# A fused attention, mixer and two-layer feed-forward kernel: where the norm's small steps keep the variance, and which engine rounds the streamed weights

## The chip, the cores and the metric

One core of one Trainium2 chip runs the whole program in one launch. The metric is the device time in microseconds. Before the change three runs took 1761.98, 1762.68 and 1764.5 us, a median of 1762.68 us.

## What is computed

The inputs are `q`, `k`, `v` of shape 8 x 8 x 576 x 64 and two sets of feed-forward weights (512 to 2048 to 512). Cut to what matters here:

```python
x  = attention(q, mean8(k), mean8(v))           # per head; to 8 x 576 x 512
u  = x + token_mixer(x, U, V)
x1 = u + relu(u @ w1a) @ w2a                    # first layer
mu, var = mean(x1), mean((x1 - mu) ** 2)        # over the 512 features of a token
xn = (x1 - mu) / sqrt(var + 1e-6) * g
return x1 + relu(xn @ w1b) @ w2b                # second layer
```

The result has to match in float32. Matrix products run on operands that are split into a rounded part (type `fp32r`, the "hi" part) and the rest ("lo"): hi x hi, hi x lo and lo x hi are summed, so every operand costs a rounding copy (hi) and a subtraction (lo).

## The kernel before, in words

The 4608 tokens are 9 groups of 512. After the attention and the first half of the first layer (the trace's first 605 us or so), three passes run: pass 0 is the second half of the first layer, passes 1 and 2 are the two halves of the second layer. A pass goes over the 9 groups, and a group over 4 pairs of weight blocks; one (pass, group, pair) is a unit (`unit`, lines 1504 to 1590). A unit forms its 512 x 512 product by Strassen-like sums of seven 256-column products, called p1, p5, p6, p2, p3, p7, p4 in the order in which they run; all matmuls of these stand at L1519. Products p1, p6, p7 and p4 go to a PSUM bank `pa`, and p5, p2 and p3 to a bank `pbc`. Between them copies `s` are taken out of the banks (`snap`, L404 on ScalarE or L406 on VectorE), VectorE adds `s` back (L1577 into `pbc`, L1583 into `pa`), and `hidden` writes the relu to `hid` (ScalarE L1541, VectorE L1547). p2 can't write `pbc` before the copy `s` of p5 has been read from it, and p4 can't write `pa` before L1583 has read p7 from it. The second product of the previous unit (`second`, L1607, banks `py`) is put between these seven as filler. There are two `pa` banks, two `pbc` banks and four `py` banks.

While pass 0 runs over group g, the norm of group g-1 is computed in steps n0 to n3 (`norm`, lines 1694 to 1775); the last group's norm falls into the first group of pass 1. n1 subtracts the mean (L1742) and stores the tokens in HBM (`n_d`). n2 squares. n3 sums the squares over the features with four 2-column matmuls into a `pbc` bank (L1731), and then has small steps on 128 x 4 values: the square root (ScalarE, L1759, tile `lnd`), variance plus 1e-6 (VectorE, L1760, tile `lnv`), a reciprocal (L1761), and one correction of 1/sqrt, `r*(1.5 - 0.5*v*r*r)`: two products (L1763), a scale-and-add (L1764) and a product (L1765). The 512 factors are then stored token by token in HBM (L1769, `r_d`, 4 bytes each). Pass 2 needs them.

The weights of a pass are 4 pairs. They are fetched in `load_pair` (lines 1401 to 1459): two DMAs (L1417) bring the first matrices of a pair into the one buffer `wraw`, four sums and differences are formed (L1435, GpSimd or VectorE), and `split` (lines 546 to 558) makes the hi parts `w1h` (a copy: L404 on ScalarE, L406 on VectorE) and the lo parts `w1l` (L555, VectorE or GpSimd); the same follows for the second matrices (`w2h`, `w2l`) through the same buffer. Pairs of the next pass are fetched while the last group of this pass and the first of the next one run. In the first groups of pass 1, raw 8-byte weights of later blocks are also fetched (L737, `wraw<-wC`), decoded (L593 to L620), scaled and stored (L766), as background.

The order of all instructions on all engines is written out ahead by a list scheduler in the program (`Order.schedule`, lines 151 to 320): it simulates the five engines with a cost for each operation, gives an operation to one of the engines that it names (`engs`), and takes the oldest ready one first. Where VectorE and GpSimd both work on SBUF alone, it lets them exclude each other (`o.port`: an operation that touches no PSUM buffer). SyncE issues all of these DMAs, in that order too. Each engine works through its list in order, and waits at the head of it on semaphores.

Of the kernel before, what the change touches and what calls it, by code (L numbers as in the profile page):

```python
# [13 lines left out]
AF = mybir.ActivationFunctionType  # L14
ALU = mybir.AluOpType
# [15 lines left out]
TG = 512  # L31
# [19 lines left out]
class Ring:  # L51


    def __init__(self, pool, shape, dtype, n, name, fifo=True):
        self.pool, self.shape, self.dtype, self.n, self.name, self.fifo = pool, shape, dtype, n, name, fifo
        self.tiles, self.free, self.made, self.turn = None, [(0.0, i) for i in range(n)], 0, 0
        pool.rings.append(self)
# [34 lines left out]
PE, ACT, DVE, GP, SY = "pe", "act", "dve", "pool", "sync"  # L92
# [262 lines left out]
CW = 2  # L355
# [23 lines left out]
def c_pool(n):  # L379
    return 147 + 2.11 * n  # L380
# [42 lines left out]
class Kern:  # L423
    def __init__(self, nc, tc, aps):
        self.nc, self.tc = nc, tc
        (self.qT, self.kT, self.v, self.U, self.V, self.wA, self.g, self.wC, self.out) = aps
        self.w_raw = [self.wA, self.wC]
        self.o = Order(nc, tc)
        att = Pool("att")
        stg = Pool("stg")  # L430
        slots = Pool("slots", side="right")
        w = Pool("wres", side="right")
        b1 = Pool("b1", after=[att])
        b2 = Pool("b2", side="right", after=[w])
        ps = Pool("ps", space=PSUM)
        self.pools = [stg, att, slots, w, ps, b1, b2]
        R = self.R = {}

        def ring(pool, name, shape, dt=F32, n=1, fifo=True):
            R[name] = Ring(pool, shape, dt, n, name, fifo)  # L440

        ring(stg, "wraw", [128, 512], I64)
        ring(stg, "wx", [128, 512])
        ring(stg, "wt", [128, 512])
        ring(att, "araw", [128, 512], I64)
        ring(att, "ax", [128, 512])
        ring(att, "at", [128, 512])
        ring(att, "kbd", [128, 2, SP], n=2)
        ring(att, "q", [128, S], n=2)
        ring(att, "k", [128, S])  # L450
        ring(att, "v", [SP, 2, POOL * D])
        ring(att, "kp", [128, SP], n=2)
        ring(att, "vs", [SP, 4, D], F32R, 3)
        ring(att, "vz", [SP, 3 * D], n=2)
        ring(att, "ef", [SP, 2, S])
        ring(att, "sc", [128, 5, 2 * SP], n=2)
        ring(att, "mx", [128, 10], n=2)
        ring(att, "sm", [128, 10], n=2)
        ring(att, "eh", [SP, 2, S], F32R)
        ring(att, "el", [SP, 2, S], F32R)  # L460
        ring(att, "avt", [128, SH], n=2)
        ring(att, "xT", [128, S], n=5)
        ring(att, "xh", [128, DM], F32R, 2)
        ring(att, "xl", [128, DM], F32R, 2)
        ring(att, "gr", [128, DM], F32R)
        ring(att, "gs", [128, DM], F32R)
        ring(att, "ust", [128, 5, 128], F32R)
        ring(att, "us", [128, 5, 128])
        ring(att, "vd", [128, S // 4], F32R, 2)
        ring(att, "v1", [SP, 2, D + 1], n=2)  # L470
        ring(att, "x4", [128, DM])
        ring(att, "ut", [128, 4 * 64])
        ring(att, "vstk", [128, S], F32R)
        ring(slots, "op", [128, SLOT], F32R, 16)
        ring(slots, "hid", [128, SLOT], F32R, 8)
        for f in range(NA):
            for a in "hl":
                ring(w, f"w{a}{f}", [128, 1024], F32R)
        ring(w, "xg", [128, NCC, TG])
        ring(w, "ys", [128, TG], n=2)  # L480
        for j in range(NSL):
            pool = b1 if j < NSL - 1 else b2
            for a in "hl":
                ring(pool, f"w1{a}{j}", [128, 7, 256], F32R)
                ring(pool, f"w2{a}{j}", [128, 2, 512], F32R)
        ring(b1, "xraw", [128, NCC, TG])
        ring(b1, "t3", [128, 2, TH])
        ring(b1, "t2", [128, 2, TH])
        ring(b2, "s12", [128, TG], n=2)
        ring(b2, "s5", [128, TH], n=2)  # L490
        ring(b2, "res", [128, NCC, TG], n=2)
        ring(b2, "yt", [128, NCC, TG])
        ring(b2, "lnh", [128, TG], F32R)
        for a in ("lns", "lnq"):
            ring(b2, a, [128, TG])
        for a in ("lnv", "lnd"):
            ring(b2, a, [128, TG // 128])
        ring(ps, "pa", [128, 512], n=2)
        ring(ps, "pbc", [128, 512], n=2, fifo=False)
        ring(ps, "py", [128, 512], n=4)  # L500
# [900 lines left out]
    def load_pair(self, p, j):  # L1401

        o = self.o
        layer, f0 = PASSES[p][0], PASSES[p][1] + 2 * j
        w1 = [self.buf(f"w1{a}{j}") for a in "hl"]
        w2 = [self.buf(f"w2{a}{j}") for a in "hl"]
        self.wt[p, j] = w1, w2
        x, s, t = self.buf("wraw"), self.buf("wx"), self.buf("wt")

        def xf():  # L1410
            return x.t.bitcast(F32).rearrange("p (i n) -> p i n", i=2)

        def load(y, z):
            for i in range(2):
                o.op(
                    {SY: 450},
                    lambda e, i=i: e.dma_start(  # L1417
                        y.t.bitcast(F32).rearrange("p (i n) -> p i n", i=2)[:, i],
                        self.w_d[layer, f0 + i][:, z * 512 : z * 512 + 512],
                    ),  # L1420
                    r=[self.wd[layer, f0 + i, z]],
                    w=[(y, i)],
                    size=262144,
                )

        def put(k, n, src):
            h, l = (
                View(w, k, lambda t: t[:, k : k + n].rearrange("p k c -> p (k c)")) for w in w1
            )
            self.split(h, l, src, n * 256)  # L1430

        def comb(dst, i, key, a, b, op, extra=()):
            o.op(
                {GP: c_pool(256), DVE: c_dve(256)},
                lambda e: getattr(e, op)(dst.t[:, i * 256 : i * 256 + 256], a(), b()),  # L1435
                r=[x, *extra],
                w=[(dst, i)],
            )

        load(x, 0)  # L1440
        a11, a12 = (lambda: xf()[:, 0, :256]), (lambda: xf()[:, 0, 256:])
        a21, a22 = (lambda: xf()[:, 1, :256]), (lambda: xf()[:, 1, 256:])
        comb(s, 0, 0, a21, a22, "tensor_add")
        comb(s, 1, 1, lambda: s.t[:, :256], a11, "tensor_sub", [(s, 0)])
        comb(t, 0, 0, a11, a21, "tensor_sub")
        comb(t, 1, 1, a12, lambda: s.t[:, 256:], "tensor_sub", [(s, 1)])
        put(0, 2, View(x, 0, lambda t: t.bitcast(F32)[:, :512]))
        put(2, 1, View(x, 1, lambda t: t.bitcast(F32)[:, 768:]))
        put(3, 2, View(s, None, lambda t: t))
        put(5, 2, View(t, None, lambda t: t))  # L1450
        y = self.buf("wraw")
        load(y, 1)
        for i in range(2):
            self.split(
                View(w2[0], i, lambda t, i=i: t[:, i]),
                View(w2[1], i, lambda t, i=i: t[:, i]),
                View(y, i, lambda t, i=i: t.bitcast(F32)[:, i * 512 : i * 512 + 512]),
                512,
            )

    def group_prep(self, p, g):
# [232 lines left out]
    def norm(self, g):  # L1694
# [6 lines left out]
        nc, o = self.nc, self.o  # L1701
        x = self.res[g]
        b = {}
        nt = TG // 128
# [48 lines left out]
                o.op(eng, lambda e, q=q: e.tensor_add(s.t, s.t, q.t), r=[q], w=[s])  # L1753

        def n3():
            ps, sd, ve = mean(False), self.buf("lnd"), self.buf("lnv")
            small = {DVE: 70}
            part = lambda: ps.t[:, : CW * nt : CW]
            o.op({ACT: 150}, lambda e: e.activation(sd.t, part(), AF.Sqrt, bias=self.eps), r=[ps], w=[sd])  # L1759
            o.op({DVE: 130}, lambda e: e.tensor_scalar_add(ve.t, part(), 1e-6), r=[ps], w=[ve])  # L1760
            o.op({DVE: 95}, lambda e: e.reciprocal(sd.t, sd.t), w=[sd])  # L1761
            for _ in range(2):
                o.op(small, lambda e: e.tensor_mul(ve.t, ve.t, sd.t), r=[sd], w=[ve])  # L1763
            o.op(small, lambda e: e.tensor_scalar(ve.t, ve.t, -0.5, 1.5, op0=ALU.mult, op1=ALU.add), w=[ve])  # L1764
            o.op(small, lambda e: e.tensor_mul(sd.t, sd.t, ve.t), r=[ve], w=[sd])  # L1765
            self.rd[g] = d = Buf(None)
            o.op(
                {SY: 450},
                lambda e: e.dma_start(self.r_d[g].rearrange("o (i p) -> p (o i)", p=128), sd.t),  # L1769
                r=[sd],  # L1770
                w=[d],
                size=32768,
            )
# [121 lines left out]
```

## Time and profile before

| | |
|---|---|
| median of 3 runs | 1762.68 us |
| the profiled execution, its time | 1762.12 us |
| its span, first to last instruction | 1760.3 us |
| granted TensorE clock, mean | 0.997 |
| TensorE (PE) busy | 1731.6 us, 98% |
| VectorE (DVE) busy | 975.9 us, 55% |
| ScalarE (ACT) busy | 732.0 us, 42% |
| GpSimd (POOL) busy | 790.9 us, 45% |

Busy times are sums over the instructions of an engine; a wait at the head of an engine's list shows as idle time before the instruction that waited, with the instruction or the DMA that ended it. An instruction that waits for a memory port after it has started shows as a longer instruction instead. What an engine off the critical path waits costs nothing by itself.

### The profile page before, as it was taken

To read this page: it belongs to the slowest core of one execution; us is meant where nothing else is said; L and a number is where in the kernel's file an instruction comes from. 1 tells how busy PE (TensorE), PEld (TensorE's weight loads), DVE (VectorE), ACT (ScalarE), POOL (GpSimd) and SP (SyncE) were. 2 spreads that over 40 slices of the span, in tenths; PEclk is the share of its full clock that TensorE was granted. 3 is DMA by queue.
4 is the path that set the end of the run, shared out by engine and by line. 5 is a ranking of instruction groups with operands and counts; after the bars stand their busy time and mean duration, and the time that the engine had idled before them with its cause. 6 is when DMAs were issued, how large, how long until landed. Compare 5 with 4: busy or idle time off the path is not lost.

```text
span 1760.3 us, 27152 instructions
## 1 busy us (share of the span) xinstructions
PE 1731.6 (98%) x10257; PEld 1526.3 (87%) x10257; DVE 975.9 (55%) x1834; ACT 732.0 (42%) x1843; POOL 790.9 (45%) x682
## 2 busy tenths in 40 slices
PE   7999999999999999999999999999999999999998
PEld 6788888888888889989999888999899999999897
DVE  6998887887745344444446866553224633333333
ACT  4665655655622224444444443333333432232221
POOL 3342222322100077777777863333335455555654
PEclk9999999999999999999999999999999999999999
DMA  6664654554243244444444344331112433333322
GB/s 191 197 193 161 208 173 139 192 182 131 98 147 121 79 166 120 121 120 120 120 120 113 128 129 154 131 128 66 48 49 85 144 102 102 105 120 105 102 78 78
DMA packets 96691, 222.99 MB, mean 127 GB/s; under 512 B 15408, under 2 KB 15792, under 8 KB 90800
## 3 DMA queue, kind: packets, MB, share of 16 engines
q1 hardware_dynamic: 96416, 221.26, 39.7%
q8 instruction: 80, 1.31, 0.3%
q14 instruction: 51, 0.42, 0.1%
q10 hardware_dynamic: 144, 0.00, 0.0%
HBM read 151.85 MB, written 69.37 MB: 126 GB/s over the span
## 4 chain that ended last, share of the span: by engine, by line
PE 87%; DVE 4%; DMA 2%; issue 0%; ACT 0%; DVEq 0%; SPq 0%; ACTq 0%
PE py L1607 33%; PE pa L1519 17%; PE pbc L1519 12%; PE pbc L1318 10%; PE pa L1290 9%; PE py L399 2%; PE py L846 1%; DMA wraw<-wC 1%; PE py L977 1%; PE py L978 1%; PE py L1184 0%; DMA w_d<-wx 0%; PE py L1015 0%; PE py L1014 0%; DMA xraw<-u_d 0%
## 5 line engine op out<-in xcount | busy, mean ns | idle before, releaser
L1607 PE MATMUL py<-hid,w2h 128*128 128x512 f32 x1728 | 541.3, 394 | 0.2 <-DVE hid L1547 0.2
L1607 PE MATMUL py<-hid,w2l 128*128 128x512 f32 x864 | 338.6, 392 | 0.0
L1519 PE MATMUL pa<-op,w1h 128*128 128x256 f32 x1728 | 326.1, 281 | 3.3 <-DVE pa L1583 3.0
L1519 PEld LDWEIGHTS pa<-op,w1h 128*128 128x128 f32 x1728 | 293.8, 188 | 40.2 <-DVE pa L1583 3.9
L1607 PEld LDWEIGHTS py<-hid,w2h 128*128 128x128 f32 x1728 | 273.6, 189 | 11.0 <-DVE hid L1547 0.5
L555 POOL TENSOR_TENSOR op<-xraw,op 128x512 fp32r<-128x512 f32 x130 | 171.3, 1321 | 247.5 <-ACT op L404 244.7
L1577 DVE TENSOR_TENSOR pbc<-s,pbc 128x512 f32<-128x512 f32 x108 | 75.1, 696 | 369.3 <-PE pbc L1519 369.1
L1519 PEld LDWEIGHTS pbc<-op,w1h 128*128 128x128 f32 x1296 | 220.6, 188 | 29.9 <-DVE s L406 1.8
L1519 PE MATMUL pbc<-op,w1h 128*128 128x256 f32 x1296 | 244.3, 281 | 1.4 <-DVE s L406 1.4
L1519 PE MATMUL pa<-op,w1l 128*128 128x256 f32 x864 | 242.6, 281 | 0.0
L1607 PEld LDWEIGHTS py<-hid,w2l 128*128 128x128 f32 x864 | 162.4, 188 | 36.7
L1318 PE MATMUL pbc<-op,wh 128*128 128x512 f32 x576 | 182.0, 397 | 0.0
L1519 PE MATMUL pbc<-op,w1l 128*128 128x256 f32 x648 | 181.8, 281 | 0.0
L1290 PE MATMUL pa<-hid,wh 128*128 128x512 f32 x576 | 180.4, 394 | 0.0
L1519 PEld LDWEIGHTS pa<-op,w1l 128*128 128x128 f32 x864 | 162.9, 189 | 0.0
L1547 DVE SCALAR_TENSOR_TENSOR hid<-pa,hid 128x512 fp32r<-128x512 f32 x108 | 74.5, 689 | 121.7 <-ACT hid L1541 121.6
L1541 ACT ACTIVATE hid<-pbc 128x512 fp32r<-128x512 f32 x108 | 64.7, 599 | 183.3 <-DVE pbc L1577 182.4
L1541 ACT ACTIVATE hid<-pa 128x512 fp32r<-128x512 f32 x108 | 64.6, 598 | 174.2 <-PE pa L1519 167.9
L1473 POOL TENSOR_TENSOR t<-xraw 128x512 f32<-128x512 f32 x52 | 67.8, 1305 | 131.8 <-DMA xraw<-n_d 73.0
L1290 PEld LDWEIGHTS pa<-hid,wh 128*128 128x128 f32 x576 | 105.8, 188 | 21.4 <-DVE op L1297 0.2
L1519 PEld LDWEIGHTS pbc<-op,w1l 128*128 128x128 f32 x648 | 121.9, 188 | 0.0
L1318 PEld LDWEIGHTS pbc<-op,wh 128*128 128x128 f32 x576 | 103.8, 188 | 19.4
(210 smaller groups left out, 2939.3 us busy)
## 6 DMA issues: line engine op xcount, KB each, us to landing
xraw<-n_d SPq DMA_DIRECT2D x18, 1024.0 KB
wraw<-wC SPq DMA_DIRECT2D x32, 512.0 KB
wraw<-wA SPq DMA_DIRECT2D x24, 512.0 KB
w_d<-wx SPq DMA_DIRECT2D x48, 256.0 KB
wraw<-w_d SPq DMA_DIRECT2D x48, 256.0 KB
k<-kT SPq DMA_DIRECT2D x32, 288.0 KB
q<-qT SPq DMA_DIRECT2D x32, 288.0 KB
v<-v SPq DMA_DIRECT2D x32, 288.0 KB
```

The lines of the kernel that those rows point to most:

```text
L399: e.matmul(out, src, ident, start=first, stop=True, is_transpose=True, skip_group_check=True)
L555: lambda e: e.tensor_sub(lo(), src(), hi().bitcast(F32)),
L846: lambda e: e.matmul(ps.t[:, i : i + 2 * SP], q.t[:, QT[t] : QT[t] + 128], kbd.t.rearrange("p h n -> p (h n)"), start=True, stop=True, ski ...
L977: e.matmul(ps.t[:, :SH], w, eh.t[:, h, c], start=True, stop=False)
L1290: e.matmul(ps.t, w.t[:, c], u.t, start=(i == 0), stop=(i == 3 * NCC - 1))
L1318: e.matmul(ps.t, w.t[:, c], x.t, start=(f == 0 and j == 0), stop=(f == NA - 1 and j == 2))
L1473: o.op(on, lambda e: e.tensor_sub(dst(), a(), c()), r=r, w=w)
L1519: e.matmul(bank.t[:, sl], w.t[:, self.WCOL[k], c], u.t[:, t], start=(first and i == 0), stop=(last and i == 5), skip_group_check=True,)
L1541: lambda e: e.activation(h.t[:, :TG], bank.t, AF.Relu),
L1547: lambda e: e.scalar_tensor_tensor(l.t[:, :TG], bank.t, 0.0, h.t[:, :TG].bitcast(F32), op0=ALU.max, op1=ALU.subtract),
L1577: o.op({DVE: c_dve(TG)}, lambda e: e.tensor_add(c.t, s.t, c.t), r=[s], w=[c])
L1607: e.matmul(y.t, w.t[:, i, c], x.t[:, :TG], start=(first and q == 0), stop=(last and q == 2))
```

## The change

Two edits. In n3 the tile `lnv` is gone: the variance plus 1e-6, the two products and the scale-and-add are done in place in the PSUM bank that the matmuls L1731 wrote; the reciprocal and the last product still work on `lnd` in SBUF. The scheduler's costs of these small steps become 130 ns each. As the steps touch PSUM, they no longer count as SBUF-only operations there. In `load_pair`, the hi parts of the weights of passes 1 and 2 name ScalarE as their only engine; those of pass 0 keep the choice between ScalarE and VectorE.

```diff
@@ rings of SBUF tiles
-        for a in ("lnv", "lnd"):
-            ring(b2, a, [128, TG // 128])
+        ring(b2, "lnd", [128, TG // 128])
@@ load_pair
+        hi_on = (ACT,) if p else (ACT, DVE)
...
-            self.split(h, l, src, n * 256)
+            self.split(h, l, src, n * 256, hi_on=hi_on)
...
                 512,
+                hi_on=hi_on,
             )
@@ norm, n3
-            ps, sd, ve = mean(False), self.buf("lnd"), self.buf("lnv")
-            small = {DVE: 70}
-            part = lambda: ps.t[:, : CW * nt : CW]
-            o.op({ACT: 150}, lambda e: e.activation(sd.t, part(), AF.Sqrt, bias=self.eps), r=[ps], w=[sd])
-            o.op({DVE: 130}, lambda e: e.tensor_scalar_add(ve.t, part(), 1e-6), r=[ps], w=[ve])
-            o.op({DVE: 95}, lambda e: e.reciprocal(sd.t, sd.t), w=[sd])
+            ps, sd = mean(False), self.buf("lnd")
+            small = {DVE: 130}
+            ve = lambda: ps.t[:, : CW * nt : CW]
+            o.op({ACT: 150}, lambda e: e.activation(sd.t, ve(), AF.Sqrt, bias=self.eps), r=[ps], w=[sd])
+            o.op({DVE: 130}, lambda e: e.tensor_scalar_add(ve(), ve(), 1e-6), w=[ps])
+            o.op({DVE: 130}, lambda e: e.reciprocal(sd.t, sd.t), w=[sd])
             for _ in range(2):
-                o.op(small, lambda e: e.tensor_mul(ve.t, ve.t, sd.t), r=[sd], w=[ve])
-            o.op(small, lambda e: e.tensor_scalar(ve.t, ve.t, -0.5, 1.5, op0=ALU.mult, op1=ALU.add), w=[ve])
-            o.op(small, lambda e: e.tensor_mul(sd.t, sd.t, ve.t), r=[ve], w=[sd])
+                o.op(small, lambda e: e.tensor_mul(ve(), ve(), sd.t), r=[sd], w=[ps])
+            o.op(small, lambda e: e.tensor_scalar(ve(), ve(), -0.5, 1.5, op0=ALU.mult, op1=ALU.add), w=[ps])
+            o.op(small, lambda e: e.tensor_mul(sd.t, sd.t, ve()), r=[ps], w=[sd])
```

## Rows read from the trace of the kernel before

**Rows 1.** The page's first part: busy time of each engine.
```profile
PE 1731.6 (98%) x10257; PEld 1526.3 (87%) x10257; DVE 975.9 (55%) x1834; ACT 732.0 (42%) x1843; POOL 790.9 (45%) x682
```

**Rows 2.** Busy time by stretch (us from the start: length, busy time of each engine).
```profile
605.00:994.00 389.00, 388.43 (x2452) 350.37 (x2451) 192.48 (x312) 162.77 (x315) 281.10 (x222) 1.00 0.45 128
994.00:1080.00 86.00, 81.61 (x509) 72.61 (x509) 62.87 (x97) 35.27 (x71) 50.71 (x37) 1.00 0.45 134
1080.00:1760.00 680.00, 675.04 (x4225) 607.57 (x4223) 267.38 (x459) 220.79 (x428) 315.71 (x246) 1.00 0.29 98
```

**Rows 3.** Waits of PE from 600 us on: total, times, longest.
```profile
PE pa L1519 <- DVE pa L1583: 3.0, 2, 2.0
PE pbc L1519 <- DVE s L406: 1.4, 1, 1.4
```

**Rows 4.** Timeline of PE: start, length, instruction, idle before and its releaser.
```profile
1007.14 0.50 PE L1519 MATMUL pa<-op,w1h 128*128 128x256 f32 x2 [0.98 <-DVE pa L1583]
...
1014.66 0.50 PE L1519 MATMUL pbc<-op,w1h 128*128 128x256 f32 x2 [1.40 <-DVE s L406]
...
1021.09 0.40 PE L1519 MATMUL pa<-op,w1h 128*128 128x256 f32 x2
...
1064.38 0.50 PE L1519 MATMUL pa<-op,w1h 128*128 128x256 f32 x2 [2.02 <-DVE pa L1583]
```

**Rows 5.** Instructions on tile lnv: ns minimum/median/maximum.
```profile
L1763 DVE TENSOR_TENSOR lnv<-lnv,lnd x18: 163/1143/1250, 688.7 to 1040.9; 128x4 f32<-128x4 f32 x18
L1760 DVE TENSOR_SCALAR lnv<-pbc x9: 151/163/163, 688.4 to 1039.2; 128x4 f32<-128x4 f32 x9
L1764 DVE TENSOR_SCALAR lnv<-lnv x9: 170/1221/1253, 691.0 to 1042.0; 128x4 f32<-128x4 f32 x9
```

**Rows 6.** Groups by line and form, VectorE from 605 us: busy us, mean ns.
```profile
L1577 DVE TENSOR_TENSOR pbc<-s,pbc 128x512 f32<-128x512 f32 x108 | 75.1, 696 | 369.3 <-PE pbc L1519 369.1
L1583 DVE TENSOR_TENSOR pa<-s,pa 128x256 f32<-128x256 f32 x108 | 46.3, 428 | 51.2 <-PE pa L1519 51.0
```

**Rows 7.** Timeline of VectorE around the first two PE waits.
```profile
998.38 1.40 DVE L406 CAST w2h<-wraw 128x512 fp32r<-128x512 f32 x1
999.70 1.25 DVE L1763 TENSOR_TENSOR lnv<-lnv,lnd 128x4 f32<-128x4 f32 x1
...
1004.69 1.25 DVE L1764 TENSOR_SCALAR lnv<-lnv 128x4 f32<-128x4 f32 x1
...
1006.66 0.42 DVE L1583 TENSOR_TENSOR pa<-s,pa 128x256 f32<-128x256 f32 x1
...
1009.29 1.51 DVE L1435 TENSOR_TENSOR wx<-wx,wraw 128x256 f32<-128x256 f32 x1
...
1015.13 0.68 DVE L555 TENSOR_TENSOR w1l<-wt,w1h 128x512 fp32r<-128x512 f32 x1
```

**Rows 8.** Groups by form, 900 to 1440 us: weight roundings on VectorE, first and last.
```profile
L406 DVE CAST w2h<-wraw 128x512 fp32r<-128x512 f32 x10 | 7.8, 791 | 0.2 <-DMA wraw<-w_d 0.2
...
L406 DVE CAST w1h<-wx 128x512 fp32r<-128x512 f32 x2 | 0.8, 419 | 0.0
```

**Rows 9.** The same on ScalarE.
```profile
L404 ACT CAST w2h<-wraw 128x512 fp32r<-128x512 f32 x6 | 3.7, 616 | 0.5 <-DMA wraw<-w_d 0.5
```

**Rows 10.** Timeline of VectorE at the third PE wait.
```profile
1060.39 0.43 DVE L595 TENSOR_SCALAR wt<-wraw 128x512 int32<-128x512 int32 x1 [6.16 <-DMA wraw<-wC]
```

**Rows 11.** Timeline of SyncE's queue: the DMA issues around these.
```profile
1003.02 2.09 SPq L1417 DMA_DIRECT2D wraw<-w_d  x2
1006.17 0.37 SPq L1769 DMA_DIRECT2D r_d<-lnd  x1
...
1044.66 0.37 SPq L1769 DMA_DIRECT2D r_d<-lnd  x1
...
1048.35 0.33 SPq L737 DMA_DIRECT2D wraw<-wC  x1
```

**Rows 12.** Busy time by stretch behind a store of the factors; the last column is GB/s.
```profile
1046.00:1056.00 10.00, 10.00 (x64) 8.95 (x63) 4.62 (x8) 2.31 (x5) 0.12 (x1) 1.00 0.57 32
```

## The prediction

> **What bounds the kernel now.** I read the busy times first: TensorE works 98% of the span, every other engine about half or less [rows 1]. So only a hole in TensorE's work can be won, and only a new hole can be lost. The busy times by stretch say where the holes are: while pass 0 runs, and with it seven of the nine norms, TensorE is idle for 0.57 of 389 us; between 994 and 1080 us, where the last weight pairs of pass 1, the last two norms and the background decoding meet, it is idle for 4.39 of 86 us; after that for 4.96 of 680 us [rows 2], which is the drain of the output at the end, out of reach here. The waits of TensorE name the engine: VectorE's add L1583, twice, 3.0 us, and VectorE's copy of `s`, once, 1.4 us [rows 3]. The timeline places them: 0.98 us up to 1007.14, 1.40 up to 1014.66, 2.02 up to 1064.38 [rows 4]. Together 4.40 us, 0.25% of the time, and that is the most that a relieved VectorE can give. The rest of the kernel, before 686 us, sees no edited operation: the scheduler works forward in time, and the first n3 stands there.
>
> **The small steps.** In SBUF most of the products L1763 and the scale-and-add L1764 take 1.14 to 1.22 us (medians), though the shortest take 0.16 to 0.17, while L1760, which reads PSUM, never takes more than 0.163 [rows 5]. So these steps wait for something after they have started, and a PSUM operand keeps them from it. The trace of before does not show a small step that also writes PSUM. The nearest rows are L1577 and L1583, in place in PSUM with one SBUF operand: 696 ns at 512 columns, 428 at 256 [rows 6]; that is 1.05 ns a column and 0.16 us at none, so 0.164 us at 4. Below lies 0.151, the shortest L1760; above, 1.25, if the wait stayed [rows 5]. I take 0.16. Per norm at the medians that frees 2 x 0.98 + 1.06 = 3.0 us of VectorE. In pass 0 it lies beside TensorE's work, and is worth nothing there: that stretch has no hole to close.
>
> Two things are added. The first write to the bank waits for the square root, which reads it. Behind it in VectorE's list stand L1547, L1577 and L1583, so a late root holds these. Bounds: zero, where the root is done first, and 1.25 us, the longest small step as the nearest thing. I take zero, since in pass 0 TensorE didn't notice a chain longer by 3 us. And the `pbc` bank stays taken for four steps more, 4 x 0.16 = 0.65 us. The second bank covers that: a unit lasts about 10.6 us (389 us over some 37 units [rows 2]), and the next product p5 goes to the other bank. Beyond that cover each us would cost one.
>
> **The roundings.** VectorE makes 23 of the roundings of passes 1 and 2, from ten for `w2h` at 791 ns to two at 419 [rows 8]; the five groups sum to 17.1 us. ScalarE does such a copy in 616 ns [rows 9], one of the 23 half as wide, so about 14 us go to an engine that is busy for 35 of 86 us where it matters [rows 2]. Cost on the path: zero to a head-of-list wait, priced below. ScalarE is not full; what changes is who stands at the head of its list when a weight DMA is late.
>
> **First hole, 0.98 us.** L1583 ends at 1007.08; TensorE was ready at 1006.16. Ahead of it in the list stand one cast of 1.40 us, two products and a scale-and-add of 1.25 each [rows 7]. Out goes 1.40 + 3 x (1.25 - 0.16) = 4.7 us, against 0.9 wanted. Even if half of that was waiting that only passes on to the next step, the hole closes: -0.98. What is late next is p7 itself, TensorE's own work.
>
> **Second hole, 1.40 us.** Between 1007 and 1014 VectorE's list holds neither a cast nor a small step, but sums and remainders for the fourth pair, such as one of 1.51 us [rows 7]. These can only start earlier: their DMAs, issued at 1003.02 [rows 11], wait for the buffer `wraw`, which the shortened chain empties. Bounds 0 and -1.40. I take -0.7, half, since the same steps still meet GpSimd's.
>
> **Third hole, 2.02 us.** The decode stands at the head of VectorE's list for 6.16 us, until `wraw<-wC` has landed at 1060.39, with L1577 and L1583 behind it [rows 10]. That DMA was issued at 1048.35, 3.7 us behind the store of the factors at 1044.66 [rows 11], and in between little moves: 32 GB/s from 1046 to 1056 us [rows 12]. The chain of n3 ahead of the store gets up to 3.0 us shorter; the load then lands up to that much earlier, and 2.02 suffice. Bounds 0 and -2.02; I take -1.2, since the stores of the sums stand in the same queue and don't move.
>
> **New waits.** The list of this whole stretch is dealt anew, and the weight DMAs are now met at ScalarE's head. The one such wait in the rows, 6.16 us, cost 2.02 [rows 4, 10]. I take 0.3 of one, +0.6; bounds zero and two of them, +4.0.
>
> The sum: -0.98 - 0.7 - 1.2 + 0.6 = -2.3 us, against the profiled execution, 1762.12 us (1760.3 of span and 1.8 around it): 1759.8. The median of the three runs is 0.56 us above that execution, so **1760.4 us** is forecast.
>
> **Rivals.** *All holes close (a).* For it: VectorE is busy for 63 of 86 us [rows 2], and gets 17 us of casts less over the two changes of pass. Against: the second hole holds no edited step. -4.40 in place of -2.3: 1758.3 us.
>
> *The room is filled again (b).* The scheduler gives sums and remainders to VectorE or GpSimd, whichever ends sooner by its costs; a VectorE that looks emptier gets more of them, and the holes stay in other places. For it: L555 and L1435 already fill the list there [rows 7]. 1762.7 us, within 1 us.
>
> *The store gets ahead of a load (c), slower.* The factors of the eighth norm are stored at 1006.17, behind the two loads of the fourth pair at 1003.02 [rows 11]. With 3 us off the chain the store can slip in front. At 1044.66 such a store was followed by 10 us of next to no traffic [rows 11, 12]. The preparation of the pair ended at 1015.81 and its unit began at 1021.09 [rows 4, 7]: 5.3 us of cover. From a delay of 5.3 us on it costs one for one; at 10 us, +4.7, and with only the first hole closed 1762.68 - 0.98 + 4.7 = 1766.4 us. Against it: the loads also move forward, since `wraw` gets free sooner, and they may keep their place.
>
> The Trainium skill (DMA: Bandwidth & Descriptors, Specifications) gives 512 B as the smallest transfer at line rate, with read-modify-write below it; the store writes 4 bytes at a time. By that page (c) is a real danger. The trace agrees at 1044.66, by the 32 GB/s behind it; at 1006.17 nothing follows closely, so it does not show there.
>
> **How the numbers follow.** The forecast 0.50, (a) 0.20, (b) 0.18, (c) 0.12. The forecast's own range, with the second and third hole at their ends and one new wait: 1758.9 to 1762.2. A measurement of this kernel can tell about 0.2%, 3.5 us, from no change, so faster means below 1759.2: all of (a) and a fifth of the forecast, 0.30. Slower means above 1766.2: half of (c) and a little of two new waits beside open holes, 0.08. Between: 0.62. The range: down to (a) less the 0.7 by which the best run lay under the median, rounded, 1757.5; up to the middle between (b) and (c) and a little more, 1765.0.
>
> **What would show it.** L1763 and L1764 at 0.16 us in all nine norms; no cast of `w1h` or `w2h` on VectorE after 900 us; the span of TensorE's idle time between 994 and 1080 us down from 4.4 to about 2; no wait of TensorE for L1583 near 1006; the stores L1769 up to 3 us earlier. Wrong: small steps that still take over a microsecond; TensorE waiting for ScalarE's `s` copies or relu behind a cast whose DMA is late; the loads of the fourth pair landing after 1012 us; or a change of TensorE's own busy time, which no edit touches.

## Result: slower by 0.85%, because a small store moved up behind a large load

| | median, us | runs | range |
|---|---|---|---|
| before | 1762.32 | 6 | 1759.46 to 1764.5 |
| after | 1778.00 | 6 | 1770.17 to 1780.53 |

The ratio is 1.0085, 95% interval [1.0071, 1.0099]: about 15 us slower, outside the range that was given (1757.5 to 1765.0). The profiled execution of after is the fastest of the six (1770.17 us, span 1768.4), and 8.05 us longer than that of before. It had a head start: the same matmul of pass 0, with the same wait of 0.34 us before it, stands at 610.03 us in the trace of before and at 605.99 in that of after, and no edited operation runs up to there (timelines of TensorE, before and after). From there to the end after loses 12.1 us, most of the median's 15.7.

```profile
610.03 0.50 PE L1519 MATMUL pa<-op,w1h 128*128 128x256 f32 x2 [0.34 <-ACT s L404]
```
```profile
605.99 0.50 PE L1520 MATMUL pa<-op,w1h 128*128 128x256 f32 x2 [0.34 <-ACT s L404]
```

The first part of the page, the busy times by stretch and TensorE's waits from 605 us on, for the kernel after (they answer to [rows 1 to 3]; lines moved by one, so L1519 is L1520 here, L1769 is L1770):

```profile
PE 1731.9 (98%) x10257; PEld 1522.2 (86%) x10257; DVE 937.0 (53%) x1819; ACT 740.6 (42%) x1859; POOL 788.3 (45%) x681
```
```profile
605.00:994.00 389.00, 384.51 (x2415) 344.56 (x2414) 167.44 (x303) 162.40 (x317) 280.90 (x221) 1.00 0.43 128
994.00:1080.00 86.00, 77.97 (x472) 68.61 (x471) 51.79 (x91) 31.83 (x65) 45.07 (x35) 0.98 0.40 126
```
```profile
PE pbc L1520 <- ACT s L404: 3.6, 1, 3.6
PE pbc L1727 <- POOL lnh L1722: 3.2, 2, 1.7
PE pa L1520 <- DVE s L406: 2.2, 1, 2.2
PE py L1608 <- ACT hid L1542: 1.9, 2, 1.6
```

VectorE lost 39 us of work and TensorE's work stayed, so the edit did what it says. But TensorE's idle time grew: from 0.57 to 4.49 us while pass 0 runs, and from 4.39 to 8.03 at the change of pass. That is 7.6 of the 12.1 us; the lower granted clock of the second stretch (0.98) is worth about 1.7 more, an estimate (0.02 x 86 us), and the rest stands in no hole that the profile shows. But for one of 2.2 us, the waits listed are for ScalarE and GpSimd, on which no step of the forecast had laid a cost in pass 0.

The small steps, instructions by line (count, ns minimum/median/maximum), are as short as forecast:

```profile
L1764 DVE TENSOR_TENSOR pbc<-pbc,lnd x18: 163/170/171, 684.8 to 1045.3; 128x4 f32<-128x4 f32 x18
```
```profile
L1765 DVE TENSOR_SCALAR pbc<-pbc x9: 170/170/171, 685.2 to 1045.5; 128x4 f32<-128x4 f32 x9
```

Now SyncE's queue in the group that begins near 857 us, first before, then after. In both, the group's 1 MB load `xraw<-u_d` comes first. Before, the store of the factors stood 4.36 us behind it and behind the load of `yt`; after, the factors are ready about 3 us earlier, and the store stands 1.37 us behind the load and ahead of `yt`:

```profile
858.24 0.52 SPq L1483 DMA_DIRECT2D xraw<-u_d  x1
861.99 0.52 SPq L1658 DMA_DIRECT2D yt<-y_d  x1
862.60 0.57 SPq L1769 DMA_DIRECT2D r_d<-lnd  x1
```
```profile
856.16 0.52 SPq L1484 DMA_DIRECT2D xraw<-u_d  x1
857.53 0.38 SPq L1770 DMA_DIRECT2D r_d<-lnd  x1
859.90 0.52 SPq L1659 DMA_DIRECT2D yt<-y_d  x1
```

ScalarE's first cast of that load, before and then after, with the idle time ahead of it: from issue to cast 5.1 us before, 10.4 after.

```profile
863.38 0.62 ACT L404 CAST op<-xraw 128x512 fp32r<-128x512 f32 x1 [1.18 <-DMA xraw<-u_d]
```
```profile
866.52 0.62 ACT L404 CAST op<-xraw 128x512 fp32r<-128x512 f32 x1 [6.35 <-DMA xraw<-u_d]
```

What the DMAs moved meanwhile (stretches of 2 us; the last two columns are the busy share and GB/s), after, and then before at the same distance from the load's issue. The store's pieces run between 860 and 862 us (544 packets under 512 B there, none in the 8 us that follow). Behind them the DMA engines stay half busy and move next to nothing:

```profile
860.00:862.00 2.00, 2.00 (x14) 1.78 (x14) 0.00 (x0) 0.17 (x1) 0.00 (x0) 1.00 0.86 202
862.00:864.00 2.00, 2.00 (x15) 1.85 (x14) 1.32 (x3) 0.00 (x0) 0.00 (x0) 1.00 0.50 54
864.00:866.00 2.00, 2.00 (x13) 1.75 (x12) 0.42 (x1) 0.00 (x0) 0.00 (x0) 1.00 0.56 38
866.00:868.00 2.00, 1.78 (x11) 1.31 (x9) 0.33 (x1) 1.48 (x3) 1.37 (x2) 1.00 0.61 28
```
```profile
864.00:866.00 2.00, 2.00 (x16) 1.87 (x15) 1.28 (x2) 0.55 (x2) 2.00 (x2) 1.00 1.00 381
```

It is the tail of the load that is late. The trace records the landing of this load in 16 parts: before, all 16 come between 862.78 and 863.36 us; after, 14 have come by 862.03, and the last two come at 865.04 and 866.50.

GpSimd waits for the same load and then is late with `lnh` of the norm, for which TensorE waits (timelines of GpSimd and of TensorE, after):

```profile
866.63 1.28 POOL L1474 TENSOR_TENSOR t<-xraw 128x512 f32<-128x512 f32 x1 [6.75 <-DMA xraw<-u_d]
...
878.63 1.26 POOL L1722 TENSOR_TENSOR lnh<-lns,lnh 64x512 fp32r<-64x512 f32 x1 [0.73 <-ACT lnh L1719]
```
```profile
879.95 0.51 PE L1727 MATMUL pbc<-lnh,ones 128*128 128x512 f32 x1 [1.70 <-POOL lnh L1722]
```

The delay is not there in every group: in the six groups whose load has a store behind it, the idle time before this cast is between 1.47 and 6.35 us (before 1.12 to 1.25). Over pass 0 it sums to 23.2 us in eight waits against 10.2 before. At the change of pass the same store stands 1.94 us behind the two weight loads of the fourth pair (before 3.15 [rows 11]), and a cast waits for them at the head of ScalarE's list, with two relus behind it. (This cast is ScalarE's alone by the second edit, but ScalarE made it before, too.) From 1006 to 1010 us the DMA engines move nothing at all, and yet the load has not landed. Later the decode's load is issued 3.57 us behind the next store, much as before [rows 10, 11]. SyncE, the stretches from 1006 us, ScalarE, VectorE and TensorE, after:

```profile
1000.81 1.89 SPq L1417 DMA_DIRECT2D wraw<-w_d  x2
1002.75 0.42 SPq L1770 DMA_DIRECT2D r_d<-lnd  x1
...
1046.82 1.08 SPq L1770 DMA_DIRECT2D r_d<-lnd  x1
...
1050.39 0.33 SPq L736 DMA_DIRECT2D wraw<-wC  x1
```
```profile
1006.00:1008.00 2.00, 2.00 (x14) 1.74 (x13) 0.59 (x2) 0.49 (x1) 1.08 (x1) 1.00 0.00 0
1008.00:1010.00 2.00, 2.00 (x16) 1.87 (x14) 0.00 (x0) 0.00 (x0) 0.00 (x0) 1.00 0.00 0
```
```profile
1010.94 0.41 ACT L404 CAST w1h<-wraw 128x256 fp32r<-128x256 f32 x1 [4.45 <-DMA wraw<-w_d]
...
1064.70 0.40 ACT L418 ACTIVATE wx<-wx,g_sb 128x128 f32<-128x128 f32 x1 [5.93 <-DVE wx L619]
```
```profile
1061.39 0.43 DVE L594 TENSOR_SCALAR wt<-wraw 128x512 int32<-128x512 int32 x1 [5.53 <-DMA wraw<-wC]
```
```profile
1011.90 0.49 PE L1608 MATMUL py<-hid,w2h 128*128 128x512 f32 x1 [1.63 <-ACT hid L1542]
...
1016.99 0.50 PE L1520 MATMUL pa<-op,w1h 128*128 128x256 f32 x2 [2.21 <-DVE s L406]
...
1065.41 0.51 PE L1520 MATMUL pbc<-op,w1h 128*128 128x256 f32 x2 [3.60 <-ACT s L404]
```

### The profile page after: what moved, and what is told of

It is laid out like the page before. It is cut to its first block, busy times and chain, and to the rows that moved or that the text cites. A ratio compares the mean times of both kernels' runs of the same rounds, so it can differ in the third digit from the quotient of the medians.

```text
span 1768.4 us, 27150 instructions
## 1 busy us (share of the span) xinstructions
PE 1731.9 (98%) x10257; PEld 1522.2 (86%) x10257; DVE 937.0 (53%) x1819; ACT 740.6 (42%) x1859; POOL 788.3 (45%) x681
## 3 DMA queue, kind: packets, MB, share of 16 engines
q8 instruction: 80, 1.31, 0.3%
## 4 chain that ended last, share of the span: by engine, by line
PE 84%; DMA 4%; DVE 3%; POOL 3%; ACT 1%; issue 1%; DVEq 0%; SPq 0%; POOLq 0%; ACTq 0%
PE py L1608 30%; PE pa L1520 15%; PE pbc L1520 12%; PE pbc L1317 11%; PE pa L1289 9%; PE py L399 2%; PE py L845 2%; DMA xraw<-u_d 1%; DMA wraw<-wC 1%; POOL op L554 1%; DMA wraw<-w_d 1%; PE py L976 1%; PE py L977 1%; PE py L1183 0%; PE py L1014 0%
## 5 line engine op out<-in xcount | busy, mean ns | idle before, releaser
L1608 PE MATMUL py<-hid,w2h 128*128 128x512 f32 x1728 | 543.3, 395 | 2.5 <-ACT hid L1542 1.9
L1608 PE MATMUL py<-hid,w2l 128*128 128x512 f32 x864 | 339.2, 393 | 0.0
L1520 PE MATMUL pa<-op,w1h 128*128 128x256 f32 x1728 | 326.8, 282 | 3.2 <-DVE s L406 2.2
L1520 PEld LDWEIGHTS pa<-op,w1h 128*128 128x128 f32 x1728 | 294.2, 189 | 41.2 <-DVE s L406 2.6
L1608 PEld LDWEIGHTS py<-hid,w2h 128*128 128x128 f32 x1728 | 273.7, 189 | 14.8 <-ACT hid L1542 2.4
L1520 PEld LDWEIGHTS pbc<-op,w1h 128*128 128x128 f32 x1296 | 220.9, 189 | 32.4 <-ACT s L404 4.0
L1520 PE MATMUL pbc<-op,w1h 128*128 128x256 f32 x1296 | 244.7, 281 | 3.6 <-ACT s L404 3.6
L1520 PE MATMUL pa<-op,w1l 128*128 128x256 f32 x864 | 242.4, 281 | 0.0
L1608 PEld LDWEIGHTS py<-hid,w2l 128*128 128x128 f32 x864 | 162.5, 188 | 36.8
L1520 PE MATMUL pbc<-op,w1l 128*128 128x256 f32 x648 | 181.8, 280 | 0.0
L1520 PEld LDWEIGHTS pa<-op,w1l 128*128 128x128 f32 x864 | 163.1, 189 | 0.0
L1520 PEld LDWEIGHTS pbc<-op,w1l 128*128 128x128 f32 x648 | 122.3, 189 | 0.0
```

The costliest lines, as they stand in the source:

```text
L1520: e.matmul(bank.t[:, sl], w.t[:, self.WCOL[k], c], u.t[:, t], start=(first and i == 0), stop=(last and i == 5), skip_group_check=True,)
L1608: e.matmul(y.t, w.t[:, i, c], x.t[:, :TG], start=(first and q == 0), stop=(last and q == 2))
```

## The experiments

The theory after the comparison (the store theory): 512 pieces of 4 bytes, issued right behind a large load, hold that load back; the faster small steps put them there. Its rivals: ScalarE alone for the roundings is too slow (rounding theory), or the bank that is kept longer stops TensorE (bank theory). Runs 1 to 4, 5 to 8 and 9 to 11 each share their runs of the kernel before; what is compared is the ratio to these, with its 95% interval.

**1. The PSUM steps alone.** `hi_on = (ACT, DVE)` for all passes, the rest as after.

> The norm's small steps in PSUM alone; the roundings choose between ScalarE and VectorE as before. Store theory (the factors' 4-byte store now stands right behind the group's 1 MB load, before the next load, and holds that load back; ScalarE's and GpSimd's lists wait for it, and then TensorE): this half brings the loss, 1768 to 1780 us, with ScalarE waits of 2 to 7 us for the load between 680 and 950 us. Rounding theory (the roundings at the head of ScalarE's list make the loss): 1758 to 1762 us, and no such wait. Bank theory (the pbc bank is held longer and TensorE waits for it): 1768 to 1780, but with TensorE waiting for VectorE's last small step.

1777.5 us, 1.0099 [1.0073, 1.0125]: the whole loss, without the second edit. The rounding theory falls. ScalarE's waits for `xraw<-u_d` in pass 0 are those of after (25.4 us, the longest 6.2). At the change of pass the dealt order differs: here the store, at 1002.39, stands ahead of the loads of the fourth pair, which begin at 1004.85. The cast of this pair then waits for 8.13 us, and TensorE for 5.84, up to 1018.13, behind it:

```profile
1015.89 0.62 ACT L404 CAST w1h<-wraw 128x512 fp32r<-128x512 f32 x1 [8.13 <-DMA wraw<-w_d]
```

**2. The roundings alone.** `hi_on = (ACT,) if p else (ACT, DVE)` in the kernel before.

> The roundings of passes 1 and 2 on ScalarE alone; the norm's small steps in SBUF as before, so the store keeps its place behind both loads. Store theory: 1759 to 1765 us, no wait of TensorE in pass 0. Rounding theory: 1768 to 1780 us, with the loss at the two changes of pass. Bank theory: as the store theory.

1762.12 us, 1.0006 [0.999, 1.0022]: no difference. The store keeps its place, and ScalarE waits 11.7 us for `xraw<-u_d` between 605 and 1000 us (10.2 before).

**3. The store put back.** As after, but in pass 0 the store is put behind the next group's load as a step of its own, so that SyncE issues it behind `yt`, as before (858.03 the load, 861.77 `yt`, 862.38 the store). Shortened:

```diff
+            while self.owed:                 # right behind the load of a group
+                self.owed.pop()([(x, (1, 0))])
...
+            def store(r=()):
+                o.op({SY: 450}, ..., r=[sd, *r], w=[d], size=32768)
+            if g < 9:
+                self.owed.append(store)
+            else:
+                store()
```

> The changed kernel, but the factors' store of a pass-0 group is put behind the next load again (load of the group, load of y, store), as in the kernel before; everything else as changed. Store theory: the waits of pass 0 go, and 3 to 4 us of the profiled execution's loss with them; the median falls to 1762 to 1768 us, what is left being the change of pass, where the order is still that of the changed kernel. Rounding theory and bank theory: no change, 1775 to 1780 us.

1769.14 us, 1.0052 [1.0031, 1.0073]: part of the loss is left, and the time is 1 us above the expected 1762 to 1768. Busy times by stretch of this kernel: to 950 us TensorE is idle for 0.57 of 345 us, where the kernel after was for 4.24; the loss that is left lies at the change of pass, where the store still stands right behind the weight loads (0.92 us). The longest hole there, 5.32 us, is behind the decode.

```profile
605.00:950.00 345.00, 344.43 (x2174) 309.94 (x2173) 136.63 (x262) 140.31 (x271) 246.25 (x194) 1.00 0.48 129
950.00:1090.00 140.00, 128.31 (x777) 113.84 (x776) 87.89 (x145) 59.90 (x120) 82.60 (x63) 0.96 0.40 119
```

**4. The kernel before with one more store.** Nothing of the change; a constant is stored in 512 pieces of 4 bytes, which nothing reads, right behind nine of the group loads.

```diff
             e.dma_start(x.t, src())
+            if more:
+                e.dma_start(self.j_d[...].rearrange("o (i p) -> p (o i)", p=128), self.g_sb)
```

> The kernel before, with one more 4-byte store of 512 values (of a constant, into a tensor that nobody reads) right behind each group's 1 MB load from group 2 of pass 0 to group 1 of pass 1; nothing else moved. Store theory: the load lands up to 6 us later in some groups, TensorE gets holes in pass 0, 1768 to 1785 us. Rounding and bank theory: within 0.2% of the kernel before, since no engine's work and no bank is touched.

1779.28 us, 1.0106 [1.0081, 1.0131]: the store alone brings a loss as large as that of the whole change, but not by the same path. The loads are late (ScalarE waits 24.6 us in eight waits, at most 4.2), and yet TensorE's largest waits from 605 us on are for ScalarE's copies `s`, five times in pass 0. All five go back to another transfer. In that of 2.33 us up to 755.64, the copy of 755.23 stands in ScalarE's list behind steps of the norm that wait for VectorE's L1750, and this waits until the stores `x_d<-res` have landed: 20.5 us in ten waits, of which the kernels before and after have none. This kernel has two 4-byte stores a group, the extra one and its own behind `yt`. Run 9, with one, repeats the path of after (waits of TensorE; timelines of VectorE and ScalarE):

```profile
PE pbc L1527 <- ACT s L404: 10.0, 5, 2.8
```
```profile
753.33 1.34 DVE L1750 TENSOR_TENSOR res<-res,pbc 128x512 f32<-128x512 f32 x2 [3.90 <-DMA x_d<-res]
```
```profile
754.10 0.63 ACT L1757 ACTIVATE lns<-res 128x512 f32<-128x512 f32 x1 [3.82 <-DVE res L1750]
...
755.23 0.35 ACT L404 COPY s<-pbc 128x256 f32<-128x256 f32 x1
```

**5. The store in fewer pieces, at the same place.** As after, with each partition's four factors written as one piece: 128 pieces of 16 bytes, 2 KB as before. The load that reads the factors back for pass 2 is left as it is, so they reach the wrong tokens; the run serves for its time alone.

```diff
-self.r_d[g].rearrange("o (i p) -> p (o i)", p=128), sd.t
+self.r_d[g].rearrange("o (p i) -> p (o i)", p=128), sd.t
```

> The kernel after with one change: the store of a norm's factors writes 128 pieces of 16 bytes in place of 512 pieces of 4 bytes, from the same place in SyncE's queue. The factors so land in another order of tokens, so the second layer is computed with the wrong factors; instructions, order and bytes are those of the kernel after. Theory A (the small pieces of the store, behind the group's load in the queue, delay that load): with a quarter of the pieces the delay falls to about a quarter; ScalarE's waits for xraw<-u_d in pass 0 fall from 23 us to about 12, TensorE's waits for lnh and hid (5 us) go, and the time comes to 1760 to 1766 us. Theory B (the place in the queue matters, any store that stands there holds the load): waits and time stay as in the kernel after, 1770 to 1780 us.

1756.7 us, 0.997 [0.9958, 0.9981]: by the ratios about 20 us less than after, by one access pattern, with the same bytes in the same place of the queue, and even below the 1760 to 1766 us of theory A. That any store there would hold the load (B) falls.

**6 to 8. Sixteen pieces.** The factors are transposed in 32 x 32 blocks and stored by four DMAs of 4 rows of 128 bytes: with the kernel after (6), with the PSUM steps and both engines for the roundings (7), and with the kernel before (8). Shortened:

```diff
+            o.op({DVE: 130}, lambda e: e.transpose(tt.t, sd.t), r=[sd], w=[tt])
...
+                dst = self.r_d[g].rearrange("o (i b q) -> b (o i) q", b=4, q=32)
+                for k in range(4):
+                    e.dma_start(dst[k], tt.t[32 * k : 32 * k + nt])
```

> The kernel after with its factors transposed in 32 x 32 blocks on VectorE (one more VectorE step and one GpSimd memset for a norm) and stored by four DMAs of 4 rows of 128 bytes: 16 pieces in place of 512, at the same place in SyncE's queue, right behind the group's load. Theory A (the number of small pieces): TensorE's holes in pass 0 and the long waits for the loads go although the store keeps its early place, 1757 to 1763 us. Theory B (place in the queue, whatever the pieces): with four stores there it is as slow or slower, 1770 us or more. If the two edits themselves had another cost, such as the PSUM bank or ScalarE's roundings, 1765 us or more with holes that are not behind a late load.

> As the run before it, the PSUM steps with the 16-piece store, but the rounded parts of all passes are again copied by ScalarE or VectorE. Theory A: 1757 to 1763 us, within 2 us of the run before it, as the choice of the engine for the roundings was worth nothing in the earlier pair. Theory B: 1770 us or more. If ScalarE's roundings are what makes the change of pass late, this one is faster than the run before it by 3 us or more, with less waiting of TensorE between 994 and 1090 us.

> The kernel before (small steps in SBUF, both engines for the roundings) with the 16-piece store and the transpose that it needs. It is the partner of the run before it: the two differ in the small steps alone. Theory A: the store of before stands mostly behind both loads and costs little there, so 1759 to 1763 us; against the run before it, what the faster small steps are worth when their store disturbs nothing: by the prediction's terms for the holes between 994 and 1080 us 1 to 4 us, and nothing in pass 0. Theory B: 1765 us or more, since three more stores stand in the queue.

| | median, us | ratio to before |
|---|---|---|
| 6: both edits | 1757.88 | 0.9975 [0.9963, 0.9986] |
| 7: PSUM steps | 1756.12 | 0.9964 [0.995, 0.9978] |
| 8: neither | 1756.80 | 0.9969 [0.9958, 0.9979] |

In 6 the store stands as early as in after, 1.65 us behind the load (SyncE's queue), and `yt` comes 3.74 us behind the load in both, yet the DMAs run on at 300 GB/s, where after they fell to 54 at about the same distance from the load's issue, and the cast waits for 1.29 us:

```profile
858.66 0.52 SPq L1485 DMA_DIRECT2D xraw<-u_d  x1
860.31 1.27 SPq L1776 DMA_DIRECT2D r_d<-lnt  x4
```
```profile
864.00:866.00 2.00, 2.00 (x15) 1.83 (x14) 0.80 (x2) 0.68 (x2) 1.90 (x2) 1.00 0.87 300
```
```profile
863.99 0.62 ACT L404 CAST op<-xraw 128x512 fp32r<-128x512 f32 x1 [1.29 <-DMA xraw<-u_d]
```

At the change of pass TensorE is busy for 85.67 of 86 us in 6 and for 83.61 in 8 (busy times by stretch):

```profile
994.00:1080.00 86.00, 85.67 (x536) 76.90 (x536) 55.52 (x96) 36.10 (x70) 50.58 (x40) 1.00 0.40 137
```
```profile
994.00:1080.00 86.00, 83.61 (x523) 74.59 (x523) 63.15 (x101) 36.50 (x74) 48.63 (x37) 1.00 0.42 141
```

In 8 the third hole is gone by the wider store alone, without the edits: the decode's load is issued at 1044.73 and VectorE waits 0.17 us for it, 5.8 us behind its issue, where before it took 12.0 [rows 10, 11]. The first two holes still stand there, 1.08 and 1.31 us.

```profile
1050.49 0.43 DVE L596 TENSOR_SCALAR wt<-wraw 128x512 int32<-128x512 int32 x1 [0.17 <-DMA wraw<-wC]
```

In 6 one of 0.33 us is left of the two, in 7 none. So the edits close these two holes, as the forecast said, once the store is harmless (each in one execution). In time the three can't be told apart: what the edit itself is worth lies within their intervals. The store in the kernel before cost about 5.5 us too, by the medians (8 against before: 0.31%); the trace of 8 shows about 2 of these, the third hole. Run 8's expectation, 1759 to 1763 us, missed that, and so did that of run 7 by 1 us.

**9 to 11. Number or size of the pieces.** Runs 5 to 8 changed both. Kernel 8 with an extra store behind nine loads, as in 4, of three forms (shortened; `j` is the tensor that nobody reads):

```diff
+ 9:  e.dma_start(j.rearrange("o (i p) -> p (o i)", p=128), self.ident[:, :4])
+ 10: e.dma_start(j.rearrange("o p -> p o"), self.ident[:, :1])
+ 11: e.dma_start(j.rearrange("o (i p k) -> p (o i) k", p=128, k=4), self.ident[:, :16]...)
```

> The kernel before with the 16-piece store of the factors, and right behind each load of a group (groups 2 to 8 of pass 0, 0 and 1 of pass 1) an extra store of a constant, that nothing reads, in 512 pieces of 4 bytes. The base takes 1756.8 us. If such a store costs as much as in the kernel before (17 us for nine of them), 1772 to 1778 us; it is the reference for the two runs beside it.

> The same, with the extra store in 128 pieces of 4 bytes. Theory A1 (the number of pieces sets the delay): about as the base, 1756 to 1761 us, as 128 pieces of 16 bytes were cheap. Theory A2 (pieces of 4 bytes are what is slow, and 16 bytes are not): a loss that one sees, 1764 us or more.

> The same, with the extra store in 512 pieces of 16 bytes, 8 KB in all. Theory A1 (the number of pieces): as slow as with 512 pieces of 4 bytes, 1772 to 1778 us. Theory A2 (the size of a piece): about as the base, 1756 to 1762 us.

| | median, us | ratio to before | over kernel 8's 0.9969 |
|---|---|---|---|
| 9: 512 of 4 bytes | 1767.92 | 1.0042 [1.0024, 1.006] | 0.73% |
| 10: 128 of 4 bytes | 1762.10 | 1.0003 [0.9987, 1.0019] | 0.34% |
| 11: 512 of 16 bytes | 1757.54 | 0.9984 [0.9969, 0.9998] | 0.15%, intervals overlap |

ScalarE's waits for the load between 605 and 1000 us (us in total, times, longest), 9, 10 and 11 (kernel 8: 11.2, 8, 2.8), and TensorE's largest in 9, the one that after has, too:

```profile
ACT op L404 <- DMA xraw<-u_d: 30.5, 8, 7.0
```
```profile
ACT op L404 <- DMA xraw<-u_d: 19.6, 8, 7.5
```
```profile
ACT op L404 <- DMA xraw<-u_d: 19.5, 8, 3.2
```
```profile
PE pbc L1735 <- POOL lnh L1730: 6.3, 4, 1.7
```

My expectation was that the number of pieces sets the delay (A1). It fell: as many pieces of 16 bytes, four times the bytes, cost little, though they delay most loads by 1 to 2 us; no wait for one exceeds 3.25 us. At 512 pieces the size decides (11 against 9, A2), and among 4-byte pieces the number counts as well (10 against 9). Kernel 9 itself came out 4 us below its expected band, with one such store a group where kernel 4 had two, and kernel 10 between its two. Kernel 10's profiled execution is its slowest, 1768.11 us, with one wait of 7.53 us: in this trace fewer 4-byte pieces hit a load less often, but no less hard. What was not run is a store whose pieces lie apart: in all of these, neighbouring addresses are written from different partitions, in small pieces, so the size of a piece and the closeness of the next one aren't told apart.

## Why the prediction was wrong

**The step that failed** is the one on the small steps: "In pass 0 it lies beside TensorE's work, and is worth nothing there: that stretch has no hole to close." Nothing was to be won there, that is true, but the chain of n3 ends in a DMA, and a chain that ends 3 us earlier issues it 3 us earlier. I followed the chain's VectorE time and not its store past the load of `yt` to a place 1.4 us behind the group's load. The term that the prediction put at nothing in pass 0 measured 3.9 us of TensorE's idle time there (0.57 to 4.49). Runs 1, 3, 9 and 5 show the cause: all of the loss with the PSUM steps alone; none of it in pass 0 with the store put back; the same waits and a loss of 0.73% from such a store without the change; none with wider pieces.

**Rival (c) had the mechanism and not the place or the price.** It named the 4-byte store, but asked whether the store gets in front of the loads, and only at the fourth pair. In run 1 it came as (c) has it: the store went in front there, and the hole of 5.84 us is near the +4.7 that (c) asked for that place. In after it got in front of `yt` alone, for which no engine waited longer, and stood behind the loads that came late in pass 0 and at the fourth pair: a place behind a load, while this is in flight, was enough. With a chance of 0.12, (c) gave 1766.4, which even the range left out; the store costs about 19 us (after and run 6, both against before: 1.0085 and 0.9975).

The Trainium skill (DMA: Bandwidth & Descriptors, Specifications) asks for at least 512 B a transfer for line rate and speaks of read-modify-write below it. I used that for (c), and it pointed the right way for 4 bytes. But it speaks of the small transfer's own rate, which no run here measures, and not of the transfers beside it. For these 512 B is no threshold in the runs: pieces of 128 and of 16 bytes, far below it too, cost little or nothing (runs 5, 6 and 11).

**The rest, step by step.**
- The sums: they come out, but for the upper end of the forecast's own range, which is 1762.3 and not 1762.2.
- Small steps at 0.16 us: right, 0.170 us. The chain from L1760 on shrank as forecast.
- Wait for the root: VectorE's waits for it sum to 1.6 us (longest 0.9); TensorE shows none. Zero was right.
- The bank held longer: no wait of TensorE for it in any trace. Right, and the bank theory fell with runs 5 to 7.
- The roundings: neutral in sum (run 2; 6 against 7). A cast at ScalarE's head did wait, 4.45 us, and held two relus; but in run 1 no such rule stood, and the loss was as large.
- First hole, L1583 at 1007: closed, but another stood 5 us behind it.
- Second hole, -0.7: the wait for `s` is still there, 2.21 us in place of 1.40, since VectorE, which makes the copy, waited 4.65 us for a relu behind the late cast. In run 6 it is 0.3.
- Third hole, -1.2: the decode still waits, 5.53 us in place of 6.16, and TensorE now 3.60 in place of 2.02, by way of ScalarE's scaling L418. "The load then lands up to that much earlier" did not come about: the chain was shorter, but began 4.7 us later (L1761 at 1043.91, L1760 before at 1039.2 [rows 5]), so the store and the load came at 1046.82 and 1050.39 against 1044.66 and 1048.35. What makes this load late is less the time of the store than its pieces, as run 8 shows.
- All holes closed, rival (a): that is run 6's trace (0.33 us left of 4.39), but only with the other store, which by itself closes the third.

After the hole of 3.60 us the granted clock fell: 0.85 of the 2.4 GHz level from 1064 to 1068 us and 0.72 from 1068 to 1072, parts of it at 1.2 GHz, where in [rows 2] it was 1.00. Two matmuls of L1608 that took 0.63 us at 1066.23 took 1.05 at 1068.28. So this hole cost some time beyond itself.

```profile
1064.00:1068.00 4.00, 2.59 (x14) 2.40 (x15) 1.34 (x5) 0.93 (x3) 0.00 (x0) 0.85 0.46 120
1068.00:1072.00 4.00, 4.00 (x19) 3.47 (x18) 2.77 (x7) 0.60 (x1) 0.00 (x0) 0.72 0.20 78
```

**Left open.** Why 4-byte pieces hold a load that was issued before them, and why only in some groups, no run here shows. The time of the pieces themselves it is not, by the trace of after: they are through within 2 us, and the late parts of the load land up to 5 us behind them. Nor do the traces show where the rest of the median lies, some 4 us, or why the first 605 us, without an edit, differ by 4 us between the executions of before and after.

## What to carry to other kernels

When a step off the critical path gets faster, follow it to the DMA that it issues, and look at which transfers are then in flight: the price can stand there even where the step's own time is worth nothing. Look at a store's piece size before its place: 2 KB in 4-byte pieces cost this kernel, by the medians, 5.5 us in its old place and about 19 in the new one, and a transpose and four stores of 128-byte rows took that away. Pieces of 16 bytes in another order of tokens did so, too, but whoever reads the factors then has to follow that order, which run 5 left out.

## What was not expected of the hardware

A store of 2 KB in 512 pieces, issued 1.4 us behind a 1 MB load, let ScalarE wait for that load for up to 6.35 us, 5 us more than in the same group before, while the DMA engines were half busy and moved 28 to 54 GB/s. Only 2 of the 16 parts in which the load lands were late. At the change of pass a load that such a store stood behind landed at 1010.9 us, 5 us behind the last transfer that the DMA engines show. The same 2 KB in 128 pieces of 16 bytes did little of this (longest wait behind such a store in run 5: 2.3 us), nor did 8 KB in 512 pieces of 16 bytes much (3.25 us). Later stores were held, too: in run 4 `x_d<-res`, by up to 4.3 us of VectorE's time.
